# One linear two-dimensional DMA in place of four to sixteen: a new split of the time index

## The chip, the core and the metric

The kernel runs on one core of a Trainium2 chip. The metric is the device time of one execution in microseconds (us). Three executions of the kernel before took 453.51, 454.85 and 457.79 us; the median, 454.85 us, is the figure that a change is held against. A fourth execution was profiled.

## The reference, cut to what matters

Two branches over 2048 tokens of width 512 are mixed by a gate per token. Branch A is a segmented softmax attention with a running memory and an output projection. Branch B is a long causal convolution per channel, whose kernel comes from 128 complex modes.

```python
def _B_ref(u, A_re, A_im, B_re, B_im, C_re, C_im, log_dt, Dskip):
    ...
    K = jnp.einsum('dn,dnl,dn->dl', Cc, P, dB).real
    ...                       # zero-pad K and u to 2 L, FFT, multiply, inverse FFT
    y = ...[:, :, 0, :L]
    return y.transpose(0, 2, 1) + u * Dskip[None, None, :]
x = A_x
g = _sigmoid((x * gate_w).sum(-1, keepdims=True))
a = _A_ref(x, A_wq, A_wk, A_wv, A_wo, A_beta)
b = _B_ref(x, B_A_re, ...)
return g * a + (1 - g) * b
```

## The kernel before, in words

**A planner orders the work.** Every step is an `op` with a due time (`key`), an estimated cost and its reads and writes. `schedule()` walks through them in a list schedule with one queue per engine (PE, ACT, DVE, POOL, and SP for all DMAs); `emit()` writes each engine's queue in that order with semaphore waits. An engine takes its queue strictly in order. A DMA is an `op` on SP whose cost in the plan is 0.06; the plan has one DMA channel that is free again after `lat`. If a cost in the plan changes, the order on every engine may change.

**The convolution is a two-level FFT.** The 2048 time steps are taken as 32 x 64. `x_level1` multiplies blocks of x by W1 (a 32-point transform) and writes the result Z, 4 MB, to DRAM (`scr_Z`), because the second level needs another index on the partitions. `tail` reads Z back into `Zx` in four quarters. For each of 16 steps t, it forms the convolution kernel's spectrum K (ten matmuls of `Dt` with `KTT`, L710), the transform of x (Fx, four matmuls of 64 columns with `M2`), their product (three DVE operations, L1244 to L1248), and the inverse second level (Fi, eight matmuls with `N1`), whose result V, 4 MB in all, goes to DRAM (`scr_V`) and comes back into `V2`. The last stage ("fin", four parts) adds u = x * D on PE with the identity matrix, then the inverse first level with `G2`, and one DVE operation (L1298) mixes the result with the attention branch, read from `scr_abuf`, into the output.

**The table KTT.** For each 128 channels c, `tables(c)` builds powers of the modes (L1141 to L1146), contracts them on PE into 20 x 16 samples (matmuls of 32 x 20), and evacuates them into `kex` (channels on partitions). `KTT` holds the same numbers with sample groups on the partitions; K of every t reads all of `KTT`, so all four c must have landed before the first K. In the kernel before, 16 small DMAs from SBUF to SBUF per c turn the layout.

**The gate.** `gate_tokens` computes g per token; at s = 3 the 2048 values go to DRAM (`scr_gbuf`) and come back in the token order of the last stage (`g4T`); a DVE operation, L899, waits for them in DVE's queue.

**Time index before.** Token l = 64 j + b; block b = 4 b4 + i, and the partition of (j, i) is 32 i + j. So each i is a DMA of its own for x, for the attention branch and for the output, and the two levels meet in DRAM with steps of 4 partitions (helper `sbp`).

Of the kernel before, what the change touches and what calls it, by code (L numbers as in the profile page):

```python
# [133 lines left out]
class Sched:  # L134
# [367 lines left out]
def fft_consts():  # L502
# [66 lines left out]
def build_kernel(nc, A_x, A_wq, A_wk, A_wv, A_wo, A_beta, B_A_re, B_A_im, B_B_re, B_B_im,  # L569
                 B_C_re, B_C_im, B_log_dt, B_Dskip, gate_w, out):  # L570
    with contextlib.ExitStack() as es:
# [37 lines left out]
        dskT = S.keep(1024, BF16)  # L609
# [63 lines left out]
        ldP = mkpool("ld", 1024, 1, 0)  # L673
        assert a <= T1, (a, T1)
# [22 lines left out]
        gbuf = nc.dram_tensor("scr_gbuf", (2048,), F32)  # L697
        Zd = nc.dram_tensor("scr_Z", (32 * 128 * 512,), BF16)
# [144 lines left out]
        dV = [DT() for _ in range(4)]  # L843
        dG = DT()

        def x_level1(xjP, zsP):
            S.tag = "xl1"
            for qd in range(4):
                xj = Tile(xjP, BF16)
                for i in range(4):  # L850
                    S.dma(lambda xj=xj, i=i: ap(xj, p0=32 * i, np_=32, dims=[[512, 4], [1, 512]]),
                          lambda qd=qd, i=i: bass.AP(x.tensor, x.offset + (16 * qd + i) * 512, [[64 * 512, 32], [4 * 512, 4], [1, 512]]),
                          131072, pw=[xj])
                for bl in range(4):
# [10 lines left out]
                    S.dma(lambda b4=b4: bass.AP(Zd, b4 * 2 * 128 * 512, [[512, 128], [128 * 512, 2], [1, 512]]),  # L865
# [14 lines left out]
        def gate_tokens(s):  # L880
# [232 lines left out]
        def tables(c):  # L1113
# [61 lines left out]
            for hf in range(2):  # L1175
# [11 lines left out]
                S.evac(lambda hf=hf: ap(kex, 16 * hf, [[32, NF], [1, 16]]), lambda P=P: ap(P, dims=[[1, NF], [NF, 16]]), 320, r=[P], pw=[kex])  # L1187
            for dq in range(4):
                for ft in range(4):
                    S.dma(lambda dq=dq, ft=ft: ap(KTT, d0 + 32 * dq, [[512, 5], [1, 32]], p0=32 * ft, np_=32),  # L1190
                          lambda dq=dq, ft=ft: ap(kex, ft * 32, [[128, 5], [1, 32]], p0=32 * dq, np_=32), 10240, r=[kex], pw=[KTT])


        def tail(k0):
# [20 lines left out]
            for t in range(16):  # L1215
# [46 lines left out]
                for pi in range(2):  # L1262
                    S.dma(lambda t=t, pi=pi: bass.AP(Vd, (2 * t + pi) * 65536, [[512, 64], [32768, 2], [1, 512]]),
# [131 lines left out]
```

## Time and profile before

| what | value |
|---|---|
| times of three executions | 453.51, 454.85, 457.79 us (median 454.85) |
| the profiled execution | 460.28 us, of which the span of the trace is 458.5 us |
| PE, DVE, ACT busy | 353.3, 310.0, 298.9 us (77%, 68%, 65% of the span) |
| mean granted TensorE clock | 0.87 of full speed |
| chain that ended last | PE 33%, ACT 24%, DVE 15%, SP's queue 12%, DMA 11% |
| DMA | 41.38 MB in 56887 packets, 54544 of them under 2 KB |

"SPq" is SP issuing a DMA: the time that SP's sequencer needs before it can take the next one. The chain of waits counts it when the work behind it waits for nothing else. A timeline row gives the start, the duration, the engine, the line (L252 is the helper that issues every DMA), the operation and its count; what stands in brackets is the idle time just before it and who ended it. In a table by windows, PEclk is the granted clock as a share of 2.4 GHz (0.5 is the level of 1.2 GHz) and the DMA share is the mean busy share of the 16 DMA engines.

### The profile page before, as it was taken

To read this page: it belongs to the slowest core of one execution; us is meant where nothing else is said; L and a number is where in the kernel's file an instruction comes from. 1 tells how busy PE (TensorE), PEld (TensorE's weight loads), DVE (VectorE), ACT (ScalarE), POOL (GpSimd) and SP (SyncE) were. 2 spreads that over 40 slices of the span, in tenths; PEclk is the share of its full clock that TensorE was granted. 3 is DMA by queue.
4 is the path that set the end of the run, shared out by engine and by line. 5 is a ranking of instruction groups with operands and counts; after the bars stand their busy time and mean duration, and the time that the engine had idled before them with its cause. 6 is when DMAs were issued, how large, how long until landed. Compare 5 with 4: busy or idle time off the path is not lost.

```text
span 458.5 us, 8760 instructions
## 1 busy us (share of the span) xinstructions
PE 353.3 (77%) x3609; PEld 149.7 (33%) x3609; DVE 310.0 (68%) x586; ACT 298.9 (65%) x389; POOL 3.2 (1%) x9
## 2 busy tenths in 40 slices
PE   4993887999884989899999990890769899970650
PEld 3341332334333434444455430450213334320110
DVE  4799799997373994399837972871366689960372
ACT  4899799888753997589798990792154745740000
POOL 1000000000000000000000000000000000000000
PEclk9996598899987997899999996796679899995675
DMA  7801010034411100000000001532683689777264
GB/s 210 227 25 48 0 46 1 24 113 142 131 41 52 46 1 1 8 11 24 23 3 12 8 1 26 206 106 39 193 262 103 149 212 216 207 186 181 47 169 106
DMA packets 56887, 41.38 MB, mean 90 GB/s; under 512 B 23312, under 2 KB 54544, under 8 KB 56592
## 3 DMA queue, kind: packets, MB, share of 16 engines
q1 hardware_dynamic: 56848, 40.83, 33.3%
q8 instruction: 28, 0.46, 0.4%
q14 instruction: 11, 0.09, 0.1%
HBM read 27.56 MB, written 12.59 MB: 88 GB/s over the span
## 4 chain that ended last, share of the span: by engine, by line
PE 33%; ACT 24%; DVE 15%; SPq 12%; DMA 11%; issue 3%; DVEq 0%; ACTq 0%
PE psum L710 33%; SPq L252 12%; ACT sb L1015 12%; ACT sb L256 3%; DMA scr_gbuf<-sb 2%; DVE sb L1146 2%; ACT sb L806 2%; DVE sb L1143 2%; DVE sb L257 2%; DVE sb L1141 2%; DMA scr_abuf<-sb 2%; DMA sb<-scr_V 2%; DMA sb<-in_A_x_dram 1%; ACT sb L259 1%; DMA sb<-in_A_wq_dram 1%
## 5 line engine op out<-in xcount | busy, mean ns | idle before, releaser
L710 PE MATMUL psum<-sb 128*32 128x20 bf16 (+14 forms) x3393 | 337.8, 282 | 83.0 <-ACT sb L1015 18.6
L710 PEld LDWEIGHTS psum<-sb 128*32 128x32 bf16 (+4 forms) x3393 | 134.1, 97 | 282.0 <-issue 120.0
L1015 ACT ACTIVATE sb<-psum 128x1024 bf16<-128x1024 f32 x160 | 156.0, 1030 | 18.9 <-PE psum L710 18.0
L256 ACT ACTIVATE sb<-psum 128x512 bf16<-128x512 f32 (+4 forms) x110 | 83.3, 769 | 81.9 <-PE psum L710 75.8
L257 DVE CAST sb<-psum 128x512 bf16<-128x512 f32 (+2 forms) x50 | 46.0, 922 | 49.9 <-PE psum L710 49.9
L1146 DVE TENSOR_TENSOR sb<-sb 128x512 bf16<-128x512 bf16 (+3 forms) x52 | 34.7, 667 | 1.4
L1141 DVE TENSOR_TENSOR sb<-sb 128x512 bf16<-128x512 bf16 (+3 forms) x52 | 35.3, 679 | 0.5
L1143 DVE TENSOR_TENSOR sb<-sb 128x512 bf16<-128x512 bf16 (+3 forms) x52 | 34.9, 672 | 0.0
L1298 DVE SCALAR_TENSOR_TENSOR sb<-psum,sb 128x512 bf16<-128x512 f32 x16 | 11.0, 745 | 22.5 <-PE psum L710 18.0
L259 ACT ACTIVATE sb<-psum,sb 128x512 bf16<-128x512 f32 x28 | 19.0, 693 | 9.8 <-DMA scr_abuf<-sb 6.9
L1024 DVE TENSOR_TENSOR sb<-sb 128x512 bf16<-128x512 bf16 (+1 forms) x40 | 14.2, 365 | 7.0 <-ACT sb L1015 6.7
L260 DVE TENSOR_SCALAR sb<-psum,sb 128x512 bf16<-128x512 f32 x20 | 14.9, 746 | 2.2 <-PE psum L710 2.1
L806 ACT ACTIVATE sb<-sb 128x1024 bf16<-128x1024 f32 x11 | 11.7, 1064 | 0.0
L1053 PE MATMUL psum<-sb 128*128 128x128 bf16 x128 | 11.4, 241 | 0.1
L1244 DVE TENSOR_TENSOR sb<-sb 128x1024 bf16<-128x1024 bf16 x16 | 11.1, 692 | 0.6
L1248 DVE TENSOR_TENSOR sb<-sb 128x1024 bf16<-128x1024 bf16 x16 | 11.1, 692 | 0.6
L1061 DVE TENSOR_TENSOR sb<-psum,sb 128x512 bf16<-128x512 bf16 x16 | 11.1, 691 | 0.5
L1058 DVE RECIPROCAL sb<-psum 128x32 f32<-128x32 bf16 x16 | 5.7, 354 | 8.0 <-PE psum L1053 8.0
L1246 DVE TENSOR_TENSOR sb<-sb 128x1024 bf16<-128x1024 bf16 x16 | 10.9, 684 | 0.0
L1053 PEld LDWEIGHTS psum<-sb 128*128 128x128 bf16 x128 | 9.2, 110 | 3.7 <-issue 2.4
L925 DVE TENSOR_SCALAR sb<-psum 128x512 bf16<-128x512 f32 x12 | 8.3, 688 | 3.1 <-ACT sb L924 3.1
L1284 DVE TENSOR_TENSOR sb<-sb 128x2048 bf16<-128x2048 bf16 x4 | 9.1, 2288 | 1.4 <-PE psum L710 1.4
(65 smaller groups left out, 143.9 us busy)
## 6 DMA issues: line engine op xcount, KB each, us to landing
sb<-c_D SPq DMA_DIRECT2D x16, 320.0 KB, 4.1
sb<-in_A_x_dram SPq DMA_DIRECT2D x32, 128.0 KB, 3.0
scr_Z<-sb SPq DMA_DIRECT2D x16, 256.0 KB, 2.3
sb<-scr_Z SPq DMA_DIRECT2D x32, 128.0 KB, 2.7
scr_V<-sb SPq DMA_DIRECT2D x32, 128.0 KB, 3.0
sb<-scr_V SPq DMA_DIRECT2D x8, 512.0 KB, 6.3
sb<-in_A_x_dram SPq DMA_DIRECT2D x4, 512.0 KB, 4.2
scr_abuf<-sb SPq DMA_DIRECT2D x16, 128.0 KB, 1.8
```

The source lines that it names most:

```text
L252: return self.op("SP", 0.06, lambda e: e.dma_start(out(), in_(), **kw), r=r, w=w, pw=pw, key=key, lat=lat)
L256: fa = lambda e: e.activation(dst(), src(), ACT.Copy)
L257: fd = lambda e: e.tensor_copy(dst(), src())
L259: fa = lambda e: e.activation(dst(), src(), ACT.Copy, scale=scale())
L260: fd = lambda e: e.tensor_scalar(dst(), src(), scale(), None, ALU.mult)
L710: mm = lambda e, o_, l, r_, st, sp, **kw: e.matmul(o_, lhsT=l, rhs=r_, start=st, stop=sp, skip_group_check=True, **kw)
L806: op("ACT", c_act(1024), lambda e, pw=pw, zr=zr: e.activation(ap(pw, 0, [[512, 4], [128, 2], [1, 128]]), ap(zr, 0, [[128, 4], [0, 2], [1, ...
L1015: op("ACT", c_act(1024), lambda e, P=P, pT=pT: e.activation(ap(pT, n=1024), ap(P, n=1024), ACT.Exp, scale=0.25), r=[P], w=[pT])
L1053: i = e.transpose(ap(P, tb * 256 + gi * 128, n=128), ap(ra[gi], tb * 128, n=128), ap(ident, n=128))
L1141: op("DVE", c_tt(256 * n), lambda e: e.tensor_tensor(run(tile, ne, dst, 1), run(tile, ne, src, sstep), pwv(0), ALU.mult), r=rd + [pw], w=w ...
L1143: op("DVE", c_tt(256 * n), lambda e: e.tensor_tensor(run(t2, n, 0, 1), run(tile, ne, src, sstep), pwv(1), ALU.mult), r=rd + [pw], w=[t2])
L1146: op("DVE", c_tt(256 * n), lambda e: e.tensor_tensor(D_(), D_(), ap(t2, n * 128, [[-n * 128, 2], [2 * n, 64], [1, 2 * n]]), ALU.add), r=[t ...
```

## The change

Token l = 64 j + b stays, but the partition of (j, i) becomes 4 j + i, and W1, G2 and the table of samples are permuted to match. The 64 tokens from 64 j on then lie on four neighbouring partitions in DRAM order, so the DRAM side of each transfer is one row per partition. Z is laid out by partition first, V with 2 KB per partition, `V2` holds 32 whole partitions per quarter (32 KB each), and G2 becomes two full 128 x 128 matrices (cosine and sine) that are accumulated, in place of two 64-column matmuls that stand side by side on PE. `kex` goes to DRAM (`scr_K`, 160 KB per c) and comes back in four DMAs of 128 x 5 x 32 elements, 64 B runs. The cost of a DMA on SP in the plan is 0.4 in place of 0.06, so the whole order is planned anew.

| transfer | before | now |
|---|---|---|
| x for level 1, and x, attention, output in fin | 4 x 128 KB each part | 1 x 512 KB |
| Z to `Zx` | 32 x 128 KB | 4 x 1 MB |
| V to DRAM | 32 x 128 KB | 16 x 256 KB |
| `scr_V` to `V2` | 8 x 512 KB | 4 x 1 MB |
| KTT, per c | 16 x 10 KB, SBUF to SBUF | 1 x 160 KB out, 4 x 40 KB in |
| gate back | 4 x 2 KB | 1 x 8 KB |

```diff
     def dma(self, out, in_, nbytes, r=(), w=(), pw=(), key=None, slow=False, packets=0):
...
-        return self.op("SP", 0.06, lambda e: e.dma_start(out(), in_(), **kw), r=r, w=w, pw=pw, key=key, lat=lat)
+        return self.op("SP", 0.4, lambda e: e.dma_start(out(), in_(), **kw), r=r, w=w, pw=pw, key=key, lat=lat)
...
-                    S.dma(lambda b4=b4: bass.AP(Zd, b4 * 2 * 128 * 512, [[512, 128], [128 * 512, 2], [1, 512]]),
+                    S.dma(lambda b4=b4: bass.AP(Zd, b4 * 512, [[8192, 128], [1 << 20, 2], [1, 512]]),
...
-                for i in range(4):
-                    S.dma(lambda i=i: ap(g4T, p0=32 * i, np_=32, n=16), lambda i=i: bass.AP(gbuf, i, [[64, 32], [4, 16]]), 2048, r=[dG], pw=[g4T], slow=True)
+                S.dma(lambda: ap(g4T, n=16), lambda: bass.AP(gbuf, 0, [[16, 128], [1, 16]]), 8192, r=[dG], w=[g4T])
...
+            S.dma(lambda: bass.AP(Kdr, c * 81920, [[640, 128], [1, 640]]), lambda: ap(kex, n=640), 163840, r=[kex], w=[dK[c]])
             for dq in range(4):
-                for ft in range(4):
-                    S.dma(lambda dq=dq, ft=ft: ap(KTT, d0 + 32 * dq, [[512, 5], [1, 32]], p0=32 * ft, np_=32),
-                          lambda dq=dq, ft=ft: ap(kex, ft * 32, [[128, 5], [1, 32]], p0=32 * dq, np_=32), 10240, r=[kex], pw=[KTT])
+                S.dma(lambda dq=dq: ap(KTT, d0 + 32 * dq, [[512, 5], [1, 32]]),
+                      lambda dq=dq: bass.AP(Kdr, c * 81920 + dq * 20480, [[160, 128], [32, 5], [1, 32]]),
+                      40960, r=[dK[c]], pw=[KTT], packets=640)
...
             for zq in range(4):
-                for i in range(4):
-                    for c in range(2):
-                        S.dma(lambda c=c, i=i, zq=zq: sbp(Zx, 64 * c + i, 4, 16, [[512, 8], [1, 512]], zq * 4096),
-                              lambda c=c, i=i, zq=zq: bass.AP(Zd, zq * 8 * 4096 + c * 2048 + i * 512, [[256 * 512, 16], [4096, 8], [1, 512]]),
-                              131072, r=[dZ], pw=[zparts[zq]], key=k0 + zq)
+                S.dma(lambda zq=zq: ap(Zx, zq * 4096, [[512, 8], [1, 512]]),
+                      lambda zq=zq: bass.AP(Zd, zq * 8 * 65536, [[512, 128], [65536, 8], [1, 512]]),
+                      1 << 20, r=[dZ], pw=[zparts[zq]], key=k0 + zq)
...
-                    for bl in range(2):
-                        S.dma(lambda bl=bl, k=k: sbp(V2, 64 * bl + k, 4, 16, [[512, 32], [1, 512]]),
-                              lambda bl=bl, k=k: bass.AP(Vd, k * 8 * 65536 + bl * 512, [[32768, 16], [1024, 32], [1, 512]]),
-                              524288, r=[dV[k]], pw=[V2])
+                    S.dma(lambda k=k: ap(V2, n=16384, p0=32 * k, np_=32), lambda k=k: bass.AP(Vd, k * 524288, [[16384, 32], [1, 16384]]),
+                          1 << 20, r=[dV[k]], pw=[V2])
...
                         mm(e, ap(P, n=512), ap(ident, n=128), ap(u, bl * 512, n=512), True, False)
-                        for par in range(2):
-                            i = mm(e, ap(P, n=512, p0=64 * par, np_=64), ap(G2T, n=64), ap(V2, (2 * b4 + par) * 512, n=512), False, True,
-                                   tile_position=(0, 64 * par))
+                        for c in range(2):
+                            i = mm(e, ap(P, n=512), ap(G2T, c * 128, n=128), ap(V2, b4 * 1024 + c * 512, n=512), False, c == 1)
```

SP's queue at the start of the tail, before (`sb<-sb` are the 16 DMAs of the last c into KTT, `c_D` the tables Dt of the steps t, `scr_Z` the reads into `Zx`):

```order
L252 DMA scr_abuf<-sb 128x512 x2
L252 DMA sb<-c_D 128x1280 x2
L252 DMA sb<-scr_Z 16x8x512 x6
L252 DMA sb<-sb 32x5x32 x16
L252 DMA sb<-scr_Z 16x8x512 x26
L252 DMA sb<-c_D 128x1280 x4
L252 DMA scr_V<-sb 64x2x512 x4
```

The same place now:

```order
L252 DMA scr_abuf<-sb 128x512 x2
L252 DMA sb<-c_D 128x1280 x2
L252 DMA scr_K<-sb 128x640
L252 DMA sb<-scr_Z 128x8x512 x4
L252 DMA sb<-c_D 128x1280 x2
L252 DMA sb<-scr_K 128x5x32 x4
L252 DMA sb<-in_A_x_dram 128x2048 x2
L252 DMA sb<-c_D 128x1280 x3
```

Before, 48 issues stand between the second `c_D` and the third; now there are 5, and the reads into KTT, which stood among the reads of Z, stand behind all of them and behind two more `c_D`.

PE's queue at the same place, before (64x512 is Fx or Fi, 128x512 in fives and tens is K, 17 x n is the attention's product with V):

```order
L710 MATMUL psum<-sb 128x256 x4
L710 MATMUL psum<-sb 64x512 x4
L710 MATMUL psum<-sb 17x512 x2
L710 MATMUL psum<-sb 17x384 x2
L710 MATMUL psum<-sb 17x128 x2
L710 MATMUL psum<-sb 128x512 x5
L710 MATMUL psum<-sb 17x256 x4
L710 MATMUL psum<-sb 128x512 x5
L710 MATMUL psum<-sb 64x512 x4
```

Now three Fx stand there, and attention follows; this is how it goes on, and the first K (128x512 x30) comes at the end of that stretch:

```order
L709 MATMUL psum<-sb 128x256 x4
L709 MATMUL psum<-sb 64x512 x4
L709 MATMUL psum<-sb 17x512 x2
L709 MATMUL psum<-sb 17x384 x2
L709 MATMUL psum<-sb 17x128 x2
L709 MATMUL psum<-sb 64x512 x8
L709 MATMUL psum<-sb 17x256 x4
L709 MATMUL psum<-sb 128x512 x2
L1050 MATMUL psum<-sb 128x128 x8
L709 MATMUL psum<-sb 128x384 x2
```

```order
L709 MATMUL psum<-sb 17x512 x2
L709 MATMUL psum<-sb 17x384 x2
L709 MATMUL psum<-sb 17x128 x2
L709 MATMUL psum<-sb 17x256 x4
L709 MATMUL psum<-sb 128x512 x30
L709 MATMUL psum<-sb 64x512 x20
```

The two attention groups that were spread between K's of the first steps (ten softmax operations of ACT) now stand between the third Fx and the first K.

SP's queue after the first c of KTT, before:

```order
L252 DMA scr_Z<-sb 128x2x512 x4
L252 DMA sb<-sb 32x5x32
L252 DMA scr_Z<-sb 128x2x512
L252 DMA sb<-sb 32x5x32 x15
L252 DMA scr_abuf<-sb 128x512 x4
```

and now:

```order
L252 DMA scr_Z<-sb 128x2x512
L252 DMA scr_K<-sb 128x640
L252 DMA scr_abuf<-sb 128x512 x2
L252 DMA sb<-scr_K 128x5x32
L252 DMA scr_Z<-sb 128x2x512
L252 DMA sb<-scr_K 128x5x32 x2
L252 DMA scr_Z<-sb 128x2x512
L252 DMA sb<-scr_K 128x5x32
L252 DMA scr_abuf<-sb 128x512 x2
L252 DMA scr_Z<-sb 128x2x512 x2
```

The first two stores of the attention branch moved ahead of the reads into KTT, and four of level 1's stores of Z now come after them.

## Rows read from the trace of the kernel before

**Rows 1.** The page's chain that ended last: share of the span by engine.
```profile
PE 33%; ACT 24%; DVE 15%; SPq 12%; DMA 11%; issue 3%; DVEq 0%; ACTq 0%
```

**Rows 2.** Timeline of SP, 296 to 345: start, us, engine, line, operation, transfer, count.
```profile
304.44 5.34 SPq L252 DMA_DIRECT2D sb<-scr_Z  x6
309.82 10.31 SPq L252 DMA_DIRECT2D sb<-sb  x16
320.18 16.68 SPq L252 DMA_DIRECT2D sb<-scr_Z  x26
336.90 2.44 SPq L252 DMA_DIRECT2D sb<-c_D  x4
```

**Rows 3.** Timeline of PE, 262 to 345: in brackets idle before and its releaser.
```profile
309.43 1.30 PE L710 MATMUL psum<-sb 32*128 32x384 bf16 x12 [0.17 <-ACT sb L1015]
323.54 10.79 PE L710 MATMUL psum<-sb 128*64 128x512 bf16 x52 [12.81 <-DMA sb<-scr_Z]
...
340.90 4.65 PE L710 MATMUL psum<-sb 128*128 128x512 bf16 x13 [3.06 <-DMA sb<-c_D]
```

**Rows 4.** Windows of the tail: window, length, busy by engine, PEclk, DMA share, GB/s.
```profile
311.00:324.00 13.00, 0.46 (x4) 0.22 (x4) 0.43 (x1) 1.12 (x2) 0.00 (x0) 0.54 0.24 54
...
386.00:414.00 28.00, 24.19 (x148) 9.43 (x145) 22.43 (x36) 16.37 (x18) 0.00 (x0) 1.00 0.79 197
sum 103.00, PE 80.50 PEld 29.61 DVE 65.10 ACT 49.78 POOL 0.00; mean PE 16.10 PEld 5.92 DVE 13.02 ACT 9.96 POOL 0.00
```

**Rows 5.** Timeline of SP after the first c of KTT.
```profile
129.87 9.67 SPq L252 DMA_DIRECT2D sb<-sb  x15
139.58 3.68 SPq L252 DMA_DIRECT2D scr_abuf<-sb  x4
```

**Rows 6.** Timeline of ACT at the same place.
```profile
141.65 1.27 ACT L259 ACTIVATE sb<-psum,sb 128x512 bf16<-128x512 f32 x2 [6.92 <-DMA scr_abuf<-sb]
```

**Rows 7.** Timeline of DVE at the gate.
```profile
284.26 0.17 DVE L899 TENSOR_SCALAR sb<-sb 128x16 f32<-128x16 f32 x1 [11.42 <-DMA sb<-scr_gbuf]
```

**Rows 8.** Timeline of all engines, 400 to the end: last V and fin.
```profile
412.39 3.65 SPq L252 DMA_DIRECT2D sb<-scr_abuf  x8
412.84 1.02 ACT L256 ACTIVATE sb<-psum 128x1024 bf16<-128x1024 f32 x1 [1.24 <-PE psum L710]
416.08 2.55 SPq L252 DMA_DIRECT2D scr_V<-sb  x4
420.46 1.21 SPq L252 DMA_DIRECT2D sb<-scr_V  x2
...
428.13 8.00 PE L710 MATMUL psum<-sb 128*128 128x512 bf16 x30 [15.33 <-DMA sb<-scr_V]
...
437.06 4.04 DVE L1298 SCALAR_TENSOR_TENSOR sb<-psum,sb 128x512 bf16<-128x512 f32 x6
...
444.28 2.73 DVE L1298 SCALAR_TENSOR_TENSOR sb<-psum,sb 128x512 bf16<-128x512 f32 x4 [3.18 <-DMA out_dram<-sb]
```

**Rows 9.** Timeline of SP, 0 to 270 and 268 to 300: the gate's DMAs.
```profile
268.50 0.38 SPq L252 DMA_DIRECT2D scr_gbuf<-sb  x1
279.87 2.58 SPq L252 DMA_DIRECT2D sb<-scr_gbuf  x4
```

**Rows 10.** Windows while Z was read, and while the last V2 was.
```profile
320.20:337.00 16.80, 12.68 (x68) 3.98 (x70) 8.04 (x14) 5.99 (x7) 0.00 (x0) 0.74 0.60 188
421.00:428.20 7.20, 0.07 (x1) 0.07 (x1) 0.00 (x0) 0.00 (x0) 0.00 (x0) 0.50 0.73 146
```

**Rows 11.** The page's groups of instructions: softmax; count, busy, mean ns.
```profile
L1015 ACT ACTIVATE sb<-psum 128x1024 bf16<-128x1024 f32 x160 | 156.0, 1030 | 18.9 <-PE psum L710 18.0
```

**Rows 12.** The page's DMA issues: count, size of each, median us to landing.
```profile
sb<-in_A_x_dram SPq DMA_DIRECT2D x4, 512.0 KB, 4.2
...
out_dram<-sb SPq DMA_DIRECT2D x16, 128.0 KB, 2.4
...
sb<-c_M SPq DMA_DIRECT2D x1, 1024.0 KB, 4.7
```

More of the change, by code (lines that the diff above doesn't have):

```diff
@@ L513, in fft_consts @@
                 pp, c = rho // 2, rho % 2
-                W1[32 * i:32 * i + 32, half, rl, i] = np.cos(ang[:, pp]) if c == 0 else -np.sin(ang[:, pp])
+                W1[np.arange(32) * 4 + i, half, rl, i] = np.cos(ang[:, pp]) if c == 0 else -np.sin(ang[:, pp])
     th = 2 * np.pi * (b[None, :, None] * (p[:, None, None] + 0.5) / 4096 + b[None, :, None] * q[None, None, :] / 64)
@@ L532, in fft_consts @@
             N1[rs, t, 1, 1] = c_
-    G2 = np.zeros((128, 64))
-    for bl in range(2):
-        for tp in range(32):
-            k, m = tp // 8, tp % 8
-            for c in range(2):
-                row = 64 * bl + (2 * m + c) * 4 + k
-                G2[row, 32 * bl:32 * bl + 32] = 2.0 / 4096 * (np.cos(ang[:, tp]) if c == 0 else -np.sin(ang[:, tp]))
+    G2 = np.zeros((128, 2, 128))
+    for tp in range(32):
+        for i in range(4):
+            G2[4 * tp + i, 0, np.arange(32) * 4 + i] = 2.0 / 4096 * np.cos(ang[:, tp])
+            G2[4 * tp + i, 1, np.arange(32) * 4 + i] = -2.0 / 4096 * np.sin(ang[:, tp])
     return W1.reshape(128, 2, 128), M2, N1, G2
@@ L553, in dft_const @@
             assert fe + ge not in where
-            where[fe + ge] = (f // 4, 32 * (f % 4) + g)
+            where[fe + ge] = (f // 4, 4 * g + f % 4)
     assert set(lq[1:].tolist()) == set(where)
@@ L608, in build_kernel @@
         betaT = S.keep(64, BF16)
-        dskT = S.keep(1024, BF16)
         growT = S.keep(128, F32)
@@ L673, in build_kernel @@
         ldP = mkpool("ld", 1024, 1, 0)
+        dskT = Tile(mkpool("dsk", 1024, 1, 0), BF16)
         assert a <= T1, (a, T1)
@@ L697, in build_kernel @@
         gbuf = nc.dram_tensor("scr_gbuf", (2048,), F32)
+        Kdr = nc.dram_tensor("scr_K", (4 * 81920,), BF16)
         Zd = nc.dram_tensor("scr_Z", (32 * 128 * 512,), BF16)
@@ L843, in build_kernel @@
         dV = [DT() for _ in range(4)]
+        dK = [DT() for _ in range(4)]
         dG = DT()
@@ L1275, in tail @@
                 aj = Tile(ajP, BF16)
[L1276 to L1282 removed]
+                S.dma(lambda xj=xj: ap(xj, n=2048), lambda gq=gq: bass.AP(x.tensor, x.offset + gq * 2048, [[8192, 128], [1, 2048]]),
+                      524288, w=[xj], key=k0 + 40)
+                S.dma(lambda aj=aj: ap(aj, n=2048), lambda gq=gq: bass.AP(abuf, gq * 2048, [[8192, 128], [1, 2048]]),
+                      524288, r=dA, w=[aj], key=k0 + 50)
                 u = Tile(uP, BF16)
@@ L1300, in tail @@
                         r=[P, aj, omg4T], pw=[ou])
-                for i in range(4):
-                    S.dma(lambda gq=gq, i=i: bass.AP(out, (16 * gq + i) * 512, [[64 * 512, 32], [4 * 512, 4], [1, 512]]),
-                          lambda ou=ou, i=i: ap(ou, p0=32 * i, np_=32, dims=[[512, 4], [1, 512]]), 131072, r=[ou])
-        def sbp(T, p0, pstep, np_, dims, off=0):
-            v = S.sb16[:]
-            st = v.ap[0][0]
-            base = (T.pool.addr + T.slot * T.pool.size) // 2
-            return bass.AP(v.tensor, v.offset + p0 * st + base + off, [[pstep * st, np_]] + [list(d) for d in dims])
+                S.dma(lambda gq=gq: bass.AP(out, gq * 2048, [[8192, 128], [1, 2048]]), lambda ou=ou: ap(ou, n=2048), 524288, r=[ou])
         S.key = 0.0
```

23 lines of the change are left out of this document (5 added, 18 removed).

## The prediction

> **What bounds the kernel now.** I read the chain of waits first: SP's queue has 12% of the span in it [rows 1], 55 us, though SP computes nothing. So I looked in SP's timeline for runs of issues, and in the timelines of PE, ACT and DVE for what waits at their ends. Four places come out of it.
>
> At the start of the tail SP issues 48 DMAs in a row, from 304.44 to 336.86, at 0.65 us each: 32 reads of Z, with the 16 small DMAs into KTT after the sixth [rows 2]. PE has nothing left at 310.73, gets its first quarter of Z at 323.54 (12.81 us idle) and then waits 3.06 us for a Dt that stood behind all 48 [rows 3]. The five windows from 311 to 414 hold 80.5 us of PE work in 103 us; the first has 0.46 us in 13, at a granted clock of 0.54, mostly the level of 1.2 GHz, against 1.00 in the last [rows 4]. This is the dearest place: issue, not bytes.
>
> After the first c of KTT, SP issues 15 copies, and only then, at 139.58, the four attention stores [rows 5]. ACT, whose next evacuation needs a buffer that such a store reads, stands 6.92 us [rows 6]. At the gate, DVE stands 11.42 us for four small reads, with the table and mask work queued behind that operation [rows 7]. At the end, eight reads of the attention branch are issued from 412.39 to 416.04, four V stores follow to 418.63, then the reads of V2 at 420.46; PE has it at 428.13 [rows 8].
>
> **The change, part by part.** The sum is made against the profiled execution: 460.28 us, 458.5 of them the span, so 1.78 around it. It is 5.4 us above the median of 454.85; I take differences from the trace and subtract them from the median.
>
> *Issues.* Does an issue cost by the DMA or by its packets? The store of the gate, 128 x 16 single elements, took SP 0.38 us; four reads back took 2.58, 0.65 each [rows 9]. So many packets do not make an issue long, and I count 0.4 to 0.65 us for each DMA of the change.
>
> *Start of the tail.* Four reads of Z leave SP in about 2.4 us, so the first 1 MB, with a landing like the 4.7 us of a constant of that size [rows 12], is there at about 309, before PE has run dry at 310.7. That removes the 12.81. What is late next is KTT: its four reads come behind 4.19 MB of Z and 0.66 MB of Dt. When Z was read in many DMAs it moved 188 GB/s at a DMA share of 0.60 [rows 10]; a full share would be 313. So 4.85 MB need 15.5 to 25.8 us; I take 18, because the engines were not full in that row, but 1 KB packets stay. The K reads themselves are 2560 runs of 64 B. No row has them from DRAM; the copies within SBUF were as many and never held up a queue that ran 10.31 us [rows 2], so 0 to 10.3 us, and I take 5. Counted from 304, KTT is there at 327, between 319.5 and 340.
>
> The planner has put cover there: two attention groups between the third Fx and the first K, ten softmax operations at 1.03 us [rows 11] with some evacuations, about 13 us of ACT, to 324. So PE waits some 3 us for KTT. For the rest of the tail I move PE's work as one block: 310.7 + 80.5 + 5 (the moved attention is bound by ACT; between 0 and 13) + 3 (KTT; between 0 and 16) + 6 (gaps of the K steps, between the 3.8 of the last window alone and 12.6, its share of all the work [rows 4]) = 405.2. The last evacuation before ended at 413.86 [rows 8]. **Gain 9**, with KTT at 340 a loss of 4, with all gaps but the 6 closed a gain of 17.
>
> *The first c of KTT.* The order now has one store to DRAM, then two attention stores at once, before any read into KTT. ACT has two softmax operations at 1.03 us [rows 11] and two copies to do before the third evacuation, and a 128 KB store lands after some 2.4 us [rows 12], so ACT should hardly stand. But SP then waits for the landing of the K store with four level-1 stores queued behind, whose buffers ACT needs. **Gain 6** of the 6.92; from 0, if a Z store takes the place of the wait, to 7.
>
> *The later c's.* Their 16 issues ran beside attention, and nobody waited; they cost nothing, and nothing comes back. The same holds for x in level 1, where one landing of 4.2 us [rows 12] replaces four issues and a landing.
>
> *The gate.* The store stays, and its 11.4 us to landing, 268.50 to 279.87 [rows 9]. Three of four reads at 0.65 go: **gain 2** (1.5 to 2.5).
>
> *The last V.* With two reads of the attention branch instead of eight (they wait for the last attention store as before) and one store per V, the issues end at about 414.9 instead of 418.63. But the same 1 MB of attention now enters the rings at once, ahead of V; at 146 to 313 GB/s it takes 3.4 to 7.2 us from 412.4, so V lands between 417.5 and 420.5: gain 0 to 3, I take 1.5. V2's read loses one issue, 0.6; its bytes per DMA engine are the same, and that row shows 0.73 share at 146 GB/s, nearly full [rows 10]. **Gain 2.**
>
> The rule that speaks against this read is in the Trainium skill, "SBUF — State Buffer", section "Door 1: The DMA port swizzle": 32 neighbouring partitions reach 8 of 16 ports, and 1 MiB into them ran at 189 GB/s. By that figure an estimate for the read is 5.5 us, less than the trace has now, so the sum would gain 1 to 2 us more; if instead the old, spread read used all ports, the new one would take twice its time, which is a rival below.
>
> *Fin.* Per block, three full matmuls replace one full and a pair side by side, so PE's ten blocks in 8.0 us [rows 8] become up to 4 us longer; DVE works 0.67 us per block there and hides part. The output is one 512 KB store per part; DVE's 3.18 us wait for the output buffer [rows 8] stays, since a landing of 512 KB (4.2 for a load) is longer than the 2.4 of 128 KB [rows 12] by what three issues less give back. **Loss 1.5** (0 to 4).
>
> Sum: 9 + 6 + 2 + 2 - 1.5 = 17.5 us. From the median: **437.3 us** (the profiled execution would be 442.8). Elsewhere the new order is a reshuffle of the same operations; I give it 4 us either way.
>
> **The rivals.**
> *A: KTT is the new wait.* Z at the slower rate and the small reads at their upper end: K starts at 340, the tail loses 4 instead of gaining 9, and the kernel takes 437.3 + 13 = 450. For it speaks that reads now stand behind 4.85 MB; against it the 13 us of moved attention.
> Behind this stands the same skill, "DMA: Bandwidth & Descriptors", section "Why small descriptors are slow (HBM only)": small packets pay when they go to HBM and not within SBUF, which is the move made here. No run here shows it yet.
>
> *B: V2 into half the ports.* The window of 7.2 us at 0.73 is 5.3 us of full engines [rows 10]; if the port doubles them, the last read is 5.3 us longer: 443. Against it: each old DMA alone covered 16 partitions in one half, so only half of the ports were in use at a time if the two ran one after the other.
>
> *C: everything is covered.* PE has no wait for KTT, the attention is not ACT-bound, PE runs at 1.00: gain 17 in the tail, 429.
>
> *D: slower.* The four K reads run one after another, each as slow as the gate's store: 2048 single elements took 11.4 us [rows 9]. Four of them are 45 us behind Z: KTT at 304 + 18 + 45 = 367, where PE, with the attention already used up, stands from 324; the remaining 72 us of PE work and 6 of gaps end at 445, 31 late. With the other gains of 8.5 the kernel takes 477. The 72 us are the 80.5 less 8 of PE's for the moved attention (its 13 of ACT less the 5 above). It decides where the loss in the tail eats the other 8.5: the loop then ends at 422, and KTT lands at about 344; later than that, the kernel is slower than now. Against it: that store writes 4 B, these reads carry 64 B in runs.
>
> *E: the issue goes by packets after all.* Then 1024 packets per read of Z take 8 times the 0.65 us, 32 reads' worth again, and nothing changes in the tail: 446. The 0.38 us [rows 9] speaks against it.
>
> **How the numbers follow.** The forecast has 0.60, A 0.14, B 0.08, C 0.09, D 0.06, E 0.03. The forecast's own range is 437 minus and plus 8, from the unknown rate and the reshuffle. Taking in C and part of A gives 424 to 450. About 1%, 4.5 us, is what can be told from no change: 450.3 to 459.4. The forecast, B, C, E and half of A lie below, 0.87; the other half of A is within, 0.07; D is above, 0.06.
>
> **What would show it.** In the new trace: PE's wait for Z at the tail's start gone and one for `scr_K` of 0 to 6 us ahead of the first K; ACT's 6.92 gone; DVE's 11.42 at about 9.5; last evacuation to PE's fin at 12 instead of 14.3; SP's share of the chain below 5%. The prediction is wrong if PE stands over 10 us before the first K, if an issue of 1 MB takes SP over 1 us, or if the attention moved together there runs far slower than 13 us.

## The result, and the profile after

The changed kernel takes **421.69 us** (median of 4 runs, 417.59 to 423.75), the kernel before 456.32 beside it (4 runs, 453.51 to 462.09): a ratio of 0.925, interval 0.915 to 0.935, or some 34 us less. Ratios, here and below, leave out executions more than 1.5% above the fastest of the same kernel; medians do not. I had forecast 437.3 with a range from 424 to 450. The sign was right; the gain was nearly twice what the sum gave, and the time lies just below the range.

The stages, cut in both profiled executions at the same instruction:

| stage | before, us | after, us | gain | predicted |
|---|---|---|---|---|
| start to the gate's store | 268.50 | 251.42 | 17.1 | 6 |
| to the first load of D | 33.95 | 30.85 | 3.1 | 2 |
| to the first product with D | 23.05 | 26.17 | -3.1 | 9 for this and the next |
| to the end of the last evacuation of V | 88.36 | 70.37 | 18.0 | |
| to the first block of fin | 14.27 | 10.99 | 3.3 | 2 |
| fin, to the end of the span | 30.37 | 26.00 | 4.4 | -1.5 |

The gains add to 42.7, not 34.6, since the profiled execution of before was 3.96 above its median of 456.32 and that of after 4.1 below its own. Three rows of the table miss: the first, the tail's pair (14.9 for 9) and fin.

The page's chain of waits of after; SP's queue is nearly gone from it (12% in [rows 1]):

```profile
PE 37%; DVE 27%; ACT 19%; DMA 11%; issue 4%; SPq 1%; DVEq 0%
```

SP's timeline at the tail's start (start, duration, engine, line, operation, transfer, count), for [rows 2]:

```profile
282.27 1.81 SPq L252 DMA_DIRECT2D sb<-c_D  x2
284.13 0.43 SPq L252 DMA_DIRECT2D scr_K<-sb  x1
284.67 8.08 SPq L252 DMA_DIRECT2D sb<-scr_Z  x4
292.79 3.38 SPq L252 DMA_DIRECT2D sb<-c_D  x2
296.22 6.85 SPq L252 DMA_DIRECT2D sb<-scr_K  x4
```

PE's timeline there, for [rows 3]: the first product with D starts after 0.56 us of "issue" and waits for no DMA.

```profile
307.56 0.32 PE L709 MATMUL psum<-sb 128*17 128x256 bf16 x4 [0.53 <-DVE sb L1021]
308.44 21.90 PE L709 MATMUL psum<-sb 128*128 128x512 bf16 x114 [0.56 <-issue]
```

Windows of after, for [rows 4] and [rows 10]: the Z reads, then the table's stages from the load of D on; the last evacuation of V starts at 377.79 and takes 1.02 us (length, busy us and instructions of PE, PEld, DVE, ACT, POOL, then granted clock, DMA share, GB/s).

```profile
284.50:300.00 15.50, 12.63 (x114) 4.86 (x116) 11.40 (x28) 12.05 (x15) 0.00 (x0) 0.89 1.00 317
282.27:308.44 26.17, 20.16 (x192) 7.91 (x189) 16.79 (x41) 21.72 (x25) 0.00 (x0) 0.92 0.81 240
308.44:378.81 70.37, 66.70 (x380) 25.04 (x380) 53.07 (x83) 39.04 (x41) 0.00 (x0) 0.96 0.65 190
378.81:389.80 10.99, 0.00 (x0) 0.00 (x1) 0.00 (x0) 0.00 (x1) 0.00 (x0) 0.50 0.72 205
389.80:415.80 26.00, 12.31 (x48) 4.63 (x48) 15.40 (x18) 0.00 (x0) 0.00 (x0) 0.76 0.36 121
```

The same two windows of before around the first product with D; they did not stand ahead of the prediction. It starts at 325.50, within the row of 52 matmuls of [rows 3]; the wait of 3.06 us at 340.90 is that of the third step:

```profile
302.45:325.50 23.05, 9.72 (x93) 3.67 (x89) 8.41 (x21) 9.66 (x11) 0.00 (x0) 0.71 0.38 106
325.50:413.86 88.36, 78.54 (x482) 29.13 (x480) 63.82 (x106) 48.65 (x52) 0.00 (x0) 0.92 0.72 191
```

Read the counts and PE's busy time: 192 matmuls stand ahead of the first product where 93 did, 20.16 us of work in place of 9.72, and 380 behind it where 482 did. The first product comes 3.1 us later behind the load of D, and the stretch from it on is 18.0 us shorter. While Z is read, with the tables Dt behind it, the DMA engines now move 317 GB/s at a share of 1.00, where 188 at 0.60 stood in [rows 10].

The last read into KTT is issued at 300.14 and lands 4.8 us later, 22.7 us behind the load of D and 3.5 us ahead of the first product.

At the first c of KTT (SP, for [rows 5]) the attention stores no longer stand behind 15 copies, and ACT's evacuation, for [rows 6], has no wait for a DMA:

```profile
118.74 0.33 SPq L252 DMA_DIRECT2D scr_K<-sb  x1
125.41 2.03 SPq L252 DMA_DIRECT2D scr_abuf<-sb  x2
127.48 0.61 SPq L252 DMA_DIRECT2D sb<-scr_K  x1
```
```profile
130.05 0.69 ACT L259 ACTIVATE sb<-psum,sb 128x512 bf16<-128x512 f32 x1
```

DVE at the gate, for [rows 7], then PE, DVE and SP in fin, for [rows 8]:

```profile
264.34 0.17 DVE L896 TENSOR_SCALAR sb<-sb 128x16 f32<-128x16 f32 x1 [8.58 <-DMA sb<-scr_gbuf]
```
```profile
389.80 9.51 PE L709 MATMUL psum<-sb 128*128 128x512 bf16 x36 [12.05 <-DMA sb<-scr_V]
...
393.52 0.75 DVE L1286 SCALAR_TENSOR_TENSOR sb<-psum,sb 128x512 bf16<-128x512 f32 x1 [0.19 <-PE psum L709]
394.19 2.28 DVE L1273 TENSOR_TENSOR sb<-sb 128x2048 bf16<-128x2048 bf16 x1
396.39 0.74 DVE L1286 SCALAR_TENSOR_TENSOR sb<-psum,sb 128x512 bf16<-128x512 f32 x1
397.05 2.28 DVE L1273 TENSOR_TENSOR sb<-sb 128x2048 bf16<-128x2048 bf16 x1
...
397.52 0.43 SPq L252 DMA_DIRECT2D out_dram<-sb  x1
...
403.14 2.73 DVE L1286 SCALAR_TENSOR_TENSOR sb<-psum,sb 128x512 bf16<-128x512 f32 x4 [1.18 <-DMA out_dram<-sb]
408.01 2.73 DVE L1286 SCALAR_TENSOR_TENSOR sb<-psum,sb 128x512 bf16<-128x512 f32 x4 [2.14 <-DMA out_dram<-sb]
```

### The profile page after: what moved, and what is told of

Its sections match the earlier page's. It is cut to its first block, busy times and chain, and to the rows that moved or that the text cites. A ratio compares the mean times of both kernels' runs of the same rounds, so it can differ in the third digit from the quotient of the medians.

```text
span 415.8 us, 8543 instructions
## 1 busy us (share of the span) xinstructions
PE 341.9 (82%) x3609; PEld 147.3 (35%) x3609; DVE 310.1 (75%) x589; ACT 297.3 (72%) x386; POOL 3.2 (1%) x9
## 4 chain that ended last, share of the span: by engine, by line
PE 37%; DVE 27%; ACT 19%; DMA 11%; issue 4%; SPq 1%; DVEq 0%
PE psum L709 36%; ACT sb L1012 11%; DVE sb L1143 4%; DVE sb L1140 4%; DVE sb L257 3%; DVE sb L1138 3%; DMA scr_gbuf<-sb 3%; ACT sb L256 2%; DMA sb<-in_A_x_dram 2%; DMA sb<-scr_V 2%; DVE sb L1273 2%; DMA out_dram<-sb 1%; DVE sb L1058 1%; SPq L252 1%; DMA sb<-in_A_wq_dram 1%
## 5 line engine op out<-in xcount | busy, mean ns | idle before, releaser
L709 PE MATMUL psum<-sb 128*32 128x20 bf16 (+13 forms) x3393 | 326.6, 274 | 54.2 <-DMA sb<-scr_V 12.1
L709 PEld LDWEIGHTS psum<-sb 128*32 128x32 bf16 (+4 forms) x3393 | 132.5, 95 | 244.2 <-issue 86.1
L1012 ACT ACTIVATE sb<-psum 128x1024 bf16<-128x1024 f32 x160 | 155.3, 1028 | 11.3 <-PE psum L709 10.4
L257 DVE CAST sb<-psum 128x512 bf16<-128x512 f32 (+2 forms) x50 | 45.1, 908 | 36.2 <-PE psum L709 35.7
L1138 DVE TENSOR_TENSOR sb<-sb 128x512 bf16<-128x512 bf16 (+3 forms) x52 | 35.3, 678 | 0.6
L1286 DVE SCALAR_TENSOR_TENSOR sb<-psum,sb 128x512 bf16<-128x512 f32 x16 | 11.2, 745 | 19.5 <-PE psum L709 16.2
L1050 PE MATMUL psum<-sb 128*128 128x128 bf16 x128 | 10.4, 228 | 0.5 <-DVE sb L257 0.2
L1050 PEld LDWEIGHTS psum<-sb 128*128 128x128 bf16 x128 | 8.2, 102 | 4.0 <-ACT sb L256 1.4
L1077 DVE TENSOR_TENSOR sb<-psum,sb 128x256 bf16<-128x256 f32 x24 | 9.1, 419 | 0.3
```

The lines of the kernel that those rows point to most:

```text
L257: fd = lambda e: e.tensor_copy(dst(), src())
L709: mm = lambda e, o_, l, r_, st, sp, **kw: e.matmul(o_, lhsT=l, rhs=r_, start=st, stop=sp, skip_group_check=True, **kw)
L1012: op("ACT", c_act(1024), lambda e, P=P, pT=pT: e.activation(ap(pT, n=1024), ap(P, n=1024), ACT.Exp, scale=0.25), r=[P], w=[pT])
L1050: i = e.transpose(ap(P, tb * 256 + gi * 128, n=128), ap(ra[gi], tb * 128, n=128), ap(ident, n=128))
L1138: op("DVE", c_tt(256 * n), lambda e: e.tensor_tensor(run(tile, ne, dst, 1), run(tile, ne, src, sstep), pwv(0), ALU.mult), r=rd + [pw], w=w ...
```

## The experiments

Twelve kernels, each timed beside the kernel before. Ratios are to the kernel before on the same chip, which took 458.2 to 458.7 us beside these twelve and 456.32 beside after; so a difference of 2 or 3 us between a median here and that of after says little, and the stages of the trace are given with it. In the kernels that divide transfers, one operation of the plan issues several DMAs, so that the order on PE, ACT and DVE stays that of after.

**The plan's cost of a DMA, alone.** The change also lets the planner count 0.4 us for an issue. The first kernel is before with that number, the second is after without it.

```diff
-        return self.op("SP", 0.06, lambda e: e.dma_start(...
+        return self.op("SP", 0.4, lambda e: e.dma_start(...
```

> The kernel before with one number changed: a DMA costs 0.4 in the plan in place of 0.06, so the order is planned anew and every DMA stays. Theory 1 (issues): the time was SP's issues and what stands behind them; 48 issues at 0.65 us still stand at the start of the tail, so the time stays within 5 us of the kernel before, 450 to 460. Theory 2 (the plan): most of the gain beyond the predicted 17.5 us came from the new order; then this alone gains 8 to 17 us, 438 to 447.

> The changed kernel with the old cost of a DMA in the plan, 0.06 in place of 0.4; all DMAs stay as changed. Theory 1 (issues): within 4 us of the changed kernel, 418 to 426. Theory 2 (the plan): 8 to 17 us slower than the changed kernel, 430 to 439.

Measured: before with the new number 452.51 us, ratio 0.985 (0.977 to 0.992); after with the old number 421.77, ratio 0.919 (0.912 to 0.926). The number is worth 1.5% where SP has many issues to place, and nothing that shows where it has few; both times lie where theory 1 put them, and theory 2, that the number makes most of the gain, falls.

**Many issues again, first try.** Z as shown, V2 in two reads, V's stores in two, x, attention and output in four.

```diff
                       1 << 20, r=[dZ], pw=[zparts[zq]], key=k0 + zq,
+                      subs=[(lambda h=h, zq=zq: ap(Zx, zq * 4096, [[512, 8], [1, 512]], p0=16 * h, np_=16), ...) for h in range(8)])
...
                           1 << 20, r=[dV[k]], pw=[V2],
+                          subs=[(lambda k=k, h=h: ap(V2, n=16384, p0=32 * k + 16 * h, np_=16), ...) for h in range(2)])
```

> The changed kernel with the same layout, the same plan and the same order on PE, ACT and DVE, but each merged transfer is issued in as many pieces as before: 8 per quarter of Z, 4 per x, attention and output, 2 per V and per V2 (KTT and the gate stay merged). Theory 1 (issues): 28 more issues at the start of the tail at about 0.6 us delay the K reads by 12 to 17 us, the last V by 2, the output by 2 to 4: 437 to 443. Theory 2 (the plan): within 5 us of the changed kernel, up to 427.

Measured: 445.42 us, ratio 0.961 (0.951 to 0.970); the two executions that the ratio counts took 439.94 and 443.24. That looked like the price of the issues, theory 1's 437 to 443. The trace says otherwise for a part of it: while Z was read the engines moved 131 GB/s at a share of 1.15, the first product with D came 42.1 us behind the load of D where after has 26.2, and the last V2 read took 11.4 us where after has 7.2. I had cut the transfers into blocks of neighbouring partitions, which neither kernel has, so two causes were mixed. The windows of this kernel (the middle of the Z reads; the V2 read):

```profile
296.00:306.00 10.00, 6.64 (x48) 2.41 (x48) 3.99 (x7) 3.51 (x4) 0.00 (x0) 0.60 1.15 131
...
407.70:419.20 11.50, 0.01 (x1) 0.02 (x2) 0.00 (x0) 0.00 (x0) 0.00 (x0) 0.50 0.71 91
```

**KTT by copies within SBUF, as before.** Each of the four reads per c becomes four copies into every fourth partition; the store to `scr_K` stays, though nothing reads it.

```diff
                       40960, r=[dK[c], kex], pw=[KTT], packets=640,
+                      subs=[(lambda dq=dq, b_=b_: kpart(d0 + 32 * dq, b_),
+                             lambda dq=dq, b_=b_: ap(kex, b_ * 160, [[32, 5], [1, 32]], p0=32 * dq, np_=32)) for b_ in range(4)])
```

> The changed kernel with the same plan and order, but each of the four reads of a c into KTT is four copies within SBUF, as before (the store of kex to DRAM stays, as a DMA that nobody needs). Theory 1 (issues): 12 more issues per c. After the first c, the third and fourth attention stores stand 12 x 0.6 = 7 us behind, of which ACT shows 3 to 6; before the first K, 7 us, of which 2 to 6 show on PE: 426 to 434. Theory 2 (the plan): within 3 us of the changed kernel.

Measured: 425.75 us, ratio 0.926 (0.920 to 0.932): 4 us more than after by the medians, 0.5 by the ratios, so the whole time can't tell. The stage of the first c can: from the fourth load of x to the fifth it takes 34.6 us, where after takes 29.9. The two later kernels with these copies take 35.3 and 35.0, the nine with the changed layout and the four reads 29.7 to 30.7. There DVE stands for a store of Z that waits behind the copies in SP's queue, which it does not in after:

```profile
138.17 1.23 DVE L262 CAST sb<-psum 128x1024 bf16<-128x1024 f32 x1 [3.03 <-DMA scr_Z<-sb]
```

In the tail the way from the load of D to the first product is 25.7 us, not longer than the 26.2 of after. So the 16 copies cost nothing there as long as Z is four reads; the 2 to 6 us that theory 1 gave for that place did not come.

**The Z reads, divided in two ways.**

```diff
                       1 << 20, r=[dZ], pw=[zparts[zq]], key=k0 + zq,
+  a:                  subs=[(lambda h=h, zq=zq: ap(Zx, zq * 4096 + h * 512, n=512), ...) for h in range(8)])   # 128 partitions each
+  b:                  subs=[(lambda i=i, c=c, zq=zq: sbp(Zx, 64 * c + i, 4, 16, [[512, 8], [1, 512]], zq * 4096), ...) ...])   # 16, every fourth
```

> The kernel after, with only the Z reads of the tail divided: eight transfers per quarter in place of one, each over all 128 partitions (128 rows of 1 KB). Theory N (the number of issues costs the tail): 32 issues hold SP for some 21 us as in the kernel with many issues, the K reads behind them are late, the first product with D comes 13 to 16 us later than in the kernel after, 434 to 438 us. Rival P (what costs is how few partitions one transfer covers): every transfer still covers 128 partitions, the rate stays near 317 GB/s, 4 MB take 13 to 14 us as before, SP needs 32 x 0.33 to 0.4 us inside that time; first product with D 0 to 3 us later, 421 to 425 us.

> The kernel after, with the Z reads divided as in the kernel before: eight transfers per quarter over 16 partitions each, every fourth partition of one half. Theory N: the same as with eight transfers over all partitions, 434 to 438 us. Rival P: the rate falls to 130 to 190 GB/s as in the kernel before and in the one with many issues, the Z reads take 21 to 30 us, first product with D 13 to 16 us later, 434 to 438 us; here N and P agree, they part over the other kernel of this pair.

Measured: a 422.05 us, ratio 0.919 (0.900 to 0.939); b 424.40, ratio 0.932 (0.919 to 0.945). Theory N falls: with 32 issues over all partitions the first product with D comes 26.8 us behind the load of D, 0.6 later than in after. P's price falls as well: with 16 spread partitions per transfer it comes at 30.7, 4.5 later and not 13 to 16, and the whole is some 3 us longer. The 16 neighbouring partitions of the first try, also 32 reads, had brought it at 42.1. SP's 32 issues take 16.3 us in a and 22.2 us in b, but PE's first product waits only 2.27 and 5.00 us, since the K reads come behind and there is other work. The Z reads of b as a window, where [rows 10] had 188 GB/s:

```profile
284.50:306.70 22.20, 17.24 (x159) 6.48 (x158) 15.30 (x37) 18.59 (x22) 0.00 (x0) 0.92 0.67 197
```

**Both at once.** Alone, the Z reads of before cost 2.7 us and the copies of before 4. This kernel has both (the edits of b and of KTT together).

> The kernel after, with two of its transfers divided as in the kernel before at once: the Z reads (32 issues over every fourth partition, 22.2 us of SP when done alone) and the KTT step (16 copies within SBUF per table in place of 4 reads from DRAM, 11.1 us of SP in the tail when done alone). Theory I (one SP queue, one cover: from the load of D to the first product with D there are some 26 us of other work, and only what SP needs beyond them costs): 22.2 + 11.1 + 2 us of SP before the last copy lands, first product with D 36 to 38 us behind the load of D in place of 26.2; with the 4 us of the first table 434 to 440 us. Rival (the costs add as measured alone, 2.3 and 4 us): 426 to 429 us.

Measured: **438.22 us**, ratio 0.957 (0.951 to 0.963); 14.8 above after by the ratios, 16.5 by the medians, not 7. The first product with D comes 37.7 us behind the load of D, within the 36 to 38 that theory I gave, and waits 9.20 us for the last copy. SP and PE of this kernel:

```profile
292.95 1.91 SPq L253 DMA_DIRECT2D sb<-c_D  x2
294.91 0.43 SPq L253 DMA_DIRECT2D scr_K<-sb  x1
295.44 21.90 SPq L255 DMA_DIRECT2D sb<-scr_Z  x32
317.38 1.06 SPq L253 DMA_DIRECT2D sb<-c_D  x2
318.49 10.45 SPq L255 DMA_DIRECT2D sb<-sb  x16
```
```profile
321.10 0.39 PE L715 MATMUL psum<-sb 128*17 128x256 bf16 x4 [0.48 <-DVE sb L1027]
330.69 1.91 PE L715 MATMUL psum<-sb 128*128 128x512 bf16 x4 [9.20 <-DMA sb<-sb]
```

One queue, one cover: PE has work to about 26 us behind the load of D. Either set of issues ends inside that or some 4 us beyond; their sum ends 11 us beyond.

**All transfers divided as before, in the order of after.** The last kernel, with x and fin's transfers in four, V's stores and reads in two (the rows of G2 follow).

```diff
                       524288, w=[xj],
+                      subs=[(lambda xj=xj, h=h: ap(xj, n=2048, p0=32 * h, np_=32), ...) for h in range(4)])
...
+                          subs=[(lambda k=k, h=h: sbp(V2, 64 * h + k, 4, 16, [[1, 16384]]), ...) for h in range(2)])
```

> The order of work of the kernel after on every engine, but all transfers divided as in the kernel before (x in 4, Z reads in 32 over every fourth partition, KTT in 16 copies within SBUF, V stores in 2, V reads in 2 over every fourth partition, x, attention and output of the last stage in 4). Their rows in DRAM stay the long ones of the kernel after, and so does G2. Theory I: as the kernel with Z and KTT divided, with 2 us more for x and 1 us for the last stage, 437 to 443 us; the 15 to 20 us that are then left to the kernel before lie in the order of the work and in the rows of 1 KB. Rival (the division of the transfers is the whole gain): 452 to 460 us.

Measured: 436.81 us, ratio 0.954 (0.948 to 0.960), just below theory I's range. So of the 34 us the division of the transfers holds 13 to 15 and the rest, about 20, lies in the order of work, the gate's one read, G2 and the longer DRAM rows together. By stages: from the load of D to the end of the last evacuation of V this kernel takes 107.3 us, where before takes 111.4 and after 96.5, so 10.8 of the 14.9 us gained there are the division. But the gate's store stands at 257.26, 11.2 us ahead of before, with every transfer divided. Windows of this kernel: that stretch of the tail, then two stages of attention with the KTT copies beside them, as short as in after.

```profile
288.57:395.90 107.33, 86.70 (x564) 33.05 (x568) 69.83 (x124) 60.76 (x65) 0.00 (x0) 0.89 0.67 183
...
151.66:179.96 28.30, 26.34 (x480) 12.62 (x484) 22.11 (x44) 25.61 (x34) 0.68 (x1) 1.00 0.07 20
179.96:232.89 52.93, 50.74 (x705) 24.83 (x708) 40.64 (x85) 46.56 (x63) 0.00 (x0) 1.00 0.08 18
```

**Fin's order on VectorE.**

```diff
-  ... r=[xj, dskbT], w=[u], key=k0 + 45)
+  ... r=[xj, dskbT], w=[u], key=k0 + (45 if gq < 2 else 80))
```

> The kernel after, with the two later products x * D of the last stage behind the first eight evictions on VectorE (in the kernel after one stands before the fourth eviction, the other before the fifth; in the kernel before both before the third). If the order on VectorE sets when the first output leaves and with it the buffer for the third part: the last stage 1 to 2 us shorter, 419 to 421 us, and going from before to after the same rule gave some 3 us. Rival (the wait for the output buffers and the third part's products decide): the last stage unchanged at 26 us, 421 to 423 us.

Measured: 418.16 us, ratio 0.912 (0.906 to 0.918); the interval reaches that of after, so the time alone proves little. The stage does: fin takes 22.7 us (394.59 to the end at 417.3) in place of 26.0; it takes 25.1 to 26.0 in the seven kernels that have fin as in after. So 2.4 to 3.3 us are this order's, more than I gave it. Its first output leaves at 399.81, 5.2 us after fin's first matmul, where after needs 7.7 (397.52) and before 12.1 (440.27). SP and DVE of this kernel:

```profile
398.00 4.04 DVE L1286 SCALAR_TENSOR_TENSOR sb<-psum,sb 128x512 bf16<-128x512 f32 x6 [0.28 <-PE psum L709]
...
399.81 0.43 SPq L252 DMA_DIRECT2D out_dram<-sb  x1
401.96 4.48 DVE L1273 TENSOR_TENSOR sb<-sb 128x2048 bf16<-128x2048 bf16 x2
...
406.36 1.40 DVE L1286 SCALAR_TENSOR_TENSOR sb<-psum,sb 128x512 bf16<-128x512 f32 x2
```

**The gate's wait, and where V is read to.**

```diff
 gate:  -  ... r=[g4T], w=[omg4T])
        +  ... r=[g4T], w=[omg4T], key=KEYS[2] + 4 * KEYS[3] + 45)
 V2:    -  S.dma(lambda k=k: ap(V2, n=16384, p0=32 * k, np_=32), ...
        +  S.dma(lambda k=k: sbp(V2, k, 4, 32, [[1, 16384]]), ...      # and the rows of G2
```

> The kernel after, with the one operation that needs the gate read back (1 - g, L896) planned for the middle of the tail, so that VectorE doesn't stand 8.6 us behind the store and read of the gate. Theory G (this wait is on the path that ends last): 3 to 7 us less, 415 to 419 us. Rival: TensorE and ScalarE make up for the wait later in the tail's start, where the Z reads set the first product with D at 26 us behind the load of D: no change, 420 to 423 us.

> The kernel after, with a quarter of V read into every fourth partition in place of 32 adjacent ones (the rows of G2 follow). Theory P (adjacent partitions limit the rate): the last read takes 4.5 to 5.5 us in place of 7.2 us, 2 to 3 us less, 418 to 420 us. Rival (the number of rows, 32 of 32 KB, limits it): 7.2 us again, 420 to 423 us.

Measured: gate 413.05 us, ratio 0.907 (0.895 to 0.918); V2 417.02, ratio 0.916 (0.904 to 0.928); both somewhat below what their theories gave. DVE runs 1 - g 17.2 us behind the gate's store, still ahead of the tail and not in its middle, where after runs it 12.9 us behind; its 8.58 us wait is gone, and the stage from that store to the load of D takes 23.90 us in place of 30.85, at a granted clock of 1.00 in place of 0.83. The V2 read into every fourth partition takes 5.4 us from issue to use in place of 7.2, theory P's size, with the same 32 rows of 32 KB, so the rival falls. From the last evacuation of V to fin this kernel takes 9.1 us, after 11.0, and six others that read V as after does 12.6 to 13.4. It is not only which partitions: with all transfers divided the same 32 partitions come in two reads of 16, and these take 7.6 us from the first issue to use (401.72 to 409.36). The two windows, gate and V2, of these two kernels:

```profile
254.49:278.39 23.90, 18.96 (x412) 9.14 (x414) 18.39 (x44) 20.16 (x28) 0.00 (x0) 1.00 0.37 112
```
```profile
387.20:392.58 5.38, 0.00 (x0) 0.13 (x2) 0.00 (x0) 0.00 (x0) 0.00 (x0) 0.50 0.53 195
```

**All of it together.** Gate, V2 and x * D as above; further the last quarter of V read in two halves and the last output in four stores.

> The kernel after with what the runs so far found: 1 - g planned for the middle of the tail (8.6 us), V read into every fourth partition (4 us), and further the two later products x * D behind the evictions of the first two parts of the last stage, the last quarter of V read in two halves, the last output stored in four pieces of 128 KB as each is ready. If the parts add, with 1 us for each of the last three: 405 to 410 us. Rival: the two that were measured overlap or the last three do nothing, 410 to 414 us.

Measured: **410.27 us**, ratio 0.896 (0.888 to 0.903), the fastest kernel here, at the border between the sum and its rival. By stages the measured parts are all there: 23.9 us from the gate's store to the load of D, 9.9 from the last evacuation of V to fin, 22.8 for fin. The two halves of the last V gave nothing that shows (9.1 with the whole read), nor did four stores of the last output (fin took 22.7 with x * D alone); in that the rival was right.

## Why the prediction was wrong, and where it was right

**The tail's start: mechanism right, a term of the sum wrong.** The 12.81 us wait for Z went. I had KTT at 327 in the old clock, 24.5 us behind the load of D; it landed at 22.7, and the first product came at 26.2, behind the moved attention. So the 3 us of waiting for KTT were nothing. The 1.00 share and 317 GB/s are the "full share" of 313 that I had worked out and not taken. What failed is the next line, "310.7 + 80.5 + 5 + 3 + 6". From the first product on it leaves 72 us of work, the 80.5 less 8 for the moved attention, and 6 of gaps, 78; it was 70.4, with 66.7 of work and 3.7 without. Before has 78.54 us of work behind its first product, so 11.8 and not 8 left that stretch: 10.4 now stand ahead of it, in what had been a hole, and the rest is in the profile beside a higher granted clock, 0.96 in place of 0.92. The term of 9 should have read 15.

**Issue, not bytes: half right.** I read [rows 2] as 48 issues at 0.65 us (they are 0.67), each costing the tail. The Z experiments show that 32 issues over all partitions cost 0.6 us at the first product and 32 over 16 spread ones 4.5, KTT's 16 nothing there, and both sets together 11.6 there and some 15 in the whole. The bound was SP's whole queue against one stretch of cover; with all transfers divided 10.8 us of the tail's gain are gone. The prediction's own sign of error, an issue of 1 MB holding SP over 1 us, did come: 8.08 us for four, the shortest 0.37 and the longest 3.90 us, while the DMA share stood at 1.00. That fits an SP that waits for full engines; no run separates it. Rival E, that packets set the issue, fell: one read of 1 MB was issued in 0.37 us.

**First c of KTT: right, 6 for 4 to 5.** ACT's 6.92 us went; undoing KTT alone gives 4.7 us back at that place. There it is DVE that stands, for a store of Z, which the prediction had named as what could take the wait's place.

**"I give it 4 us either way": the step that failed most.** The stages up to the gate's store gained 17.1 us in the two profiled executions: some 6 up to 50 us (the cuts there do not hold quite the same work), 4 in the stage with the first c, 5.2 and 1.7 in the two stages from 145.85 to 227.03. The profiled execution of after was its fastest; in seven other kernels with its order and the reads of `scr_K` the store stands at 252.0 to 255.9 us, so 12.6 to 17.1 is the gain. With all transfers divided 11.2 of it are left, so they come with the new order or with the longer DRAM rows, which that kernel kept, and not with the number of DMAs. In before, PE stood 5.42 us for a softmax, and later ran a stretch at a granted clock of 0.72; PE's row, and two windows of before:

```profile
43.87 1.46 PE L710 MATMUL psum<-sb 32*128 32x512 bf16 x6 [5.42 <-ACT sb L1015]
```
```profile
175.00:182.00 7.00, 6.94 (x61) 3.21 (x60) 3.24 (x9) 5.04 (x7) 0.00 (x0) 0.72 0.01 2
...
156.06:189.47 33.41, 30.10 (x491) 13.73 (x489) 20.88 (x44) 27.11 (x35) 0.67 (x1) 0.89 0.06 17
```

In after, no PE wait in 26 to 50 is over 1.61 us, and the stage that took 33.41 us takes 28.24 at a clock of 1.00. It takes 28.30 with all transfers divided as before, and 27.6 to 28.6 in the ten other kernels with the changed layout. In the kernel before with nothing but the new cost in the plan it takes 29.39:

```profile
156.35:185.74 29.39, 26.21 (x487) 12.76 (x488) 20.24 (x43) 24.93 (x31) 0.67 (x1) 1.00 0.06 20
```

There every DMA is that of before, so in this stage it is the order and not the DMAs, as far as one trace of before (33.41) can show it. I had compared the two orders only where the diff touches the work. Which of the planner's choices does it was not tried; it is not the cost of 0.4, since after with the old cost has the short stage too (27.60).

**The gate: right, 2 for 3.1,** with DVE's wait 8.58 where I wrote 9.5. I did not ask whether the operation had to stand there at all; moving it was worth some 8 us, 7.0 of them in that stage.

**The last V: right, 2 for 3.3 in this execution,** and 0.9 to 1.7 in the six other kernels that read V in the same way. The read itself did not get slower than in [rows 10], so rival B did not come. The Trainium skill, "SBUF — State Buffer", section "Door 1: The DMA port swizzle", has 32 neighbouring partitions on half of the ports. The traces agree with it in direction: one read into 32 neighbours took 7.2 us, one into every fourth partition 5.4.

**Fin: wrong sign, -1.5 for +4.4.** I took the third matmul for a cost. PE is not what ends last here; the first two parts' outputs are, since the third part needs their buffers (DVE's waits for `out_dram` above). In before both products x * D stand ahead of the third eviction; DVE's timeline of before:

```profile
430.46 0.75 DVE L1298 SCALAR_TENSOR_TENSOR sb<-psum,sb 128x512 bf16<-128x512 f32 x1 [0.36 <-PE psum L710]
432.22 2.29 DVE L1284 TENSOR_TENSOR sb<-sb 128x2048 bf16<-128x2048 bf16 x1 [1.01 <-PE psum L710]
434.85 2.29 DVE L1284 TENSOR_TENSOR sb<-sb 128x2048 bf16<-128x2048 bf16 x1 [0.34 <-PE psum L710]
```

In after one stands ahead of the fourth and one behind it, and the first part is done 7.3 us into fin in place of some 10.3. Putting both behind the eighth gave the same kind of gain again, 2.4 to 3.3 us. From DVE's last eviction to the end the span has 5.1 us in place of 7.4. With fin's transfers divided but their rows long, fin takes 27.0 us, so the number of its DMAs is worth 1 to 2; what rows of 4 KB in place of 1 KB give there was not tried alone.

**The rivals.** A and D needed the K reads to be late; in the tail these runs of 64 B from DRAM landed 4.8 to 7.4 us behind their issue, and PE waited for none. What stands behind A, the Trainium skill, "DMA: Bandwidth & Descriptors", section "Why small descriptors are slow (HBM only)", that transfers within SBUF do not pay for small descriptors, is shown by no run here: with copies within SBUF the first product came after 25.7 us, with reads from DRAM after 26.2. C, everything covered, was the nearest: 17 for the tail, measured 14.9.

## What to carry to other kernels

A run of issues on one DMA queue costs what it has beyond the other work in that stretch, so two harmless sets can be dear together: add them up against the cover before pricing either. When a planner sets the order, compare the whole order, and the waits and clock of stages that the diff does not touch; here they held a third of the gain. Look at any operation that waits on a DMA round trip for whether it must stand in that place of its engine's order.

## What the hardware showed that I had not expected

Transfers of the same bytes differed by which partitions one of them covered. While Z was read the engines moved 131 GB/s in reads of 16 neighbouring partitions, 197 in reads of 16 every fourth, and from 263 (eight reads per quarter) to 317 (one) in reads of all 128. A quarter of V ran at 146 GB/s over its 7.2 us into 32 neighbours, at 195 over 5.4 into every fourth partition, and took 7.6 when these came in two reads. The shortest issues of SP took 0.32 us; the four reads of 1 MB, with the DMA share at 1.00, 0.37 to 3.90.
